# Beta in four transfers from SP and ACT, five gate copies on GpSimd, and a new order of all items

## The chip, the cores and the metric

One core of one Trainium2 chip runs the whole program. The metric is the device time of one execution in microseconds (us); the time before is the median of three runs. The core has four compute engines that are named here as the profile names them: PE (matrix products; PEld is its weight load), DVE (vector), ACT (activation functions, copies), POOL (GpSimd). SP only issues DMA transfers; ACT and POOL can issue them too. Each engine works off its own queue in the order in which the program was written, and waits there for what its next instruction needs.

## The reference

Inputs are q, k, v and g (4 batches, 8 heads, 768 steps, 48 features), beta (4, 8, 768), and two weight matrices, w_in (384 x 2048) and w_out (2048 x 384). A delta rule runs along the steps, for each of the 32 heads; its output is the input of a two-layer network with a softplus between the layers.

```
k_n = k / (norm(k, axis=-1) + 1e-06)
for t in range(S):
    y[:, :, t] = g[:, :, t] * einsum('bhd,bhde->bhe', q[:, :, t], state)
    v_old = einsum('bhde,bhd->bhe', state, k_n[:, :, t])
    state = state + beta[:, :, t] * einsum('bhd,bhe->bhde', k_n[:, :, t], v[:, :, t] - v_old)
x = y.transpose(0, 2, 1, 3).reshape(B * S, H * D)
out = softplus(x @ w_in) @ w_out
```

## The kernel before

The 768 steps are cut into 12 chunks of 64. Within a chunk the rule is solved in closed form with the inverse of a lower triangular 64x64 matrix for each head; from chunk to chunk the state is handed on. Two chunks (a pair) share one inverse: chunks 0 and 1, 2 and 3, and so on.

Every piece of work is an item of a list (`add`, line 44), with the engines that may run it, what it depends on and the buffers it uses. The table `_ORDER` at the end of the file names each item with its engine (S for SP, A, D, G for POOL, P). `emit` writes the items in just that order, so the table sets the queue of every engine, and which ring slot a buffer gets. The items that matter here, by the name they have in this text:

- load: one transfer of 192 KB, half a chunk of k, v or g (L249, 64 rows of 16 heads with 192 bytes each) or of q (L271, 128 runs of 1536 bytes). All go from SP, apart from two of k that go from ACT.
- front of a chunk (L306): casts of k and q to 16 bits (chunks 0 and 1) or k times the inverse norm (kmul, L327), transposes on PE (k at L345, q at L388), their copies out of PSUM (kev, by way of the copy helper, L218 on ACT and L220 on DVE), products of k with k and q (gram: L432, L461, L503) and copies (kkc, kdc) or masked copies (mask, L480 and L518) of those.
- norms of a pair: squares (ksq, L545, ACT), sums (red, L549, DVE), then the root: on ACT for pairs 0/1 and 2/3 (L561), as a power on POOL for the others (pow, L566); eps (L570, L572, DVE).
- inverse of a pair: beta over the squared norms (lbeta, L583 to L586, pair 0/1 only), the diagonal (diag, L621), diagonal blocks picked out (kd0, kd1 at L604) and turned around (ln, L611), two preparations (prep, L629), 15 steps (L639 and L646), all of these serial; for pair 0/1 on DVE, for the others on POOL. Then a scaling (cv, L228), transposes (tn, L667; t32, L686), and three rounds of small products: xmm (L707), tmm (L732), zmm (L770), with copies xs, tlo, thi and z between.
- chain of a chunk: ks and qs (L813), w (L847), umm (L855), u1, zu (L878), u2, smm (L898), s (the new state, L913), ymm (L928), y (times g, L943), ytr (L962), xt.
- dense layers: g1 (h, L992; for chunks 0, 1, 10 and 11 an item is 6 products 256 wide and there are 8 items a chunk), softplus (L1004, ACT), g2 (L1019, four products an item), o (copy, ACT or DVE), store (L1039, SP). There are two PSUM buffers for h and one for o.
- wload: the weights in eight quarters, w0.0 to w0.3 of w_in and w1.0 to w1.3 of w_out, issued by POOL (L297), cast to 16 bits on the way. g1 needs one quarter of w_in, g2 one of w_out.
- warm: 24 items of three idle products on the identity (L1064) that keep PE busy; they need nothing but the buffer of o.
- table: one ACT instruction (L1051) that brings the softplus table in.

Beta lies in SBUF as one row of 32 steps for each of 128 partitions and six pairs. Before, eight transfers bring it in at the start, issued by POOL (L175), 16 partitions each. They stand on POOL ahead of the mask and of the constants of xs.

The queue of POOL before, after the constants:

```
c16:0 clear:2 diag:2 tlo:0.1 tlo:0.0 w0.0 cast:q5 w0.3 w0.2 w0.1 w1.0 w1.1 w1.3 pow:4 w1.2 prep:2.0 prep:2.1 step:2.0 ...
```

A name with one number after the colon is of that chunk, or of the pair that begins with it. pow:4 belongs to chunks 4 and 5, prep:2 and step:2 to 2 and 3. eps:4 follows ln:2 on DVE.

Of the kernel before, what the change touches and what calls it, by code (L numbers as in the profile page):

```python
# [11 lines left out]
F16 = mybir.dt.float16  # L12
# [62 lines left out]
def kernel(  # L75
# [11 lines left out]
    nc = tc.nc  # L87
    B, H, S, D = q.shape
    P = 128
    C = 64  # L90
    HC = 32
    NC = S // C
# [10 lines left out]
    pool = ctx.enter_context(tc.tile_pool(name="sb", bufs=1))  # L103
# [4 lines left out]
    add = prog.add  # L108
# [59 lines left out]
    for r in range(2):  # L168
        for hf in range(2):
            l0 = 32 * (2 * r + hf)  # L170
            src = beta[2 * r : 2 * r + 2].rearrange(
                "p h (c l r) -> (p h) l c r", l=2, r=64
            )
            for cl in range(2):
                nc.gpsimd.dma_start(  # L175
                    out=beta_l[l0 + 16 * cl : l0 + 16 * cl + 16],
                    in_=src[:, cl, :, 32 * hf : 32 * hf + 32],
                )
# [59 lines left out]


# [336 lines left out]
    def inverse(cc, kk, kk_it, kkd, kd_it, nv, nv_it):  # L576
# [11 lines left out]
        if raw:  # L588
            bl_it = add("lbeta", tag, "D", lbeta, deps=[nv_it], bufs=[nv, nl, bl])
            bb = [bl]  # L590
        else:
            bl_it, bb = None, []
# [5 lines left out]
        if not raw:  # L598
# [4 lines left out]
            def kd1(en):  # L603
# [21 lines left out]
                   deps=[prev, bl_it], bufs=[tt] + bb)  # L625
# [166 lines left out]

    state = [None, []]
# [249 lines left out]
    for cc in range(NC // 2):  # L1043
        cs = [2 * cc, 2 * cc + 1]
        nv, kk = Buf(r_nv), Buf(r_kk)
        nv_it = norms(cs, nv, cc in ON_ACT)
        kkd = Buf(r_kkd)
        ka, kb = front(cs[0], kk, kkd, nv, nv_it), front(cs[1], kk, kkd, nv, nv_it)
        inverse(cc, kk, ka[0] + kb[0], kkd, ka[1] + kb[1], nv, nv_it)
    table = add("table", "", "A",  # L1050
                lambda en: nc.scalar.activation(dummy, half_c[:, :1], AF.Softplus),  # L1051
                deps=[root_last[0]])
    for c in range(NC):
        chain(c)
# [20 lines left out]
S0 D158 P1232 P1234 P1233 P1235 A1 P1236 P1238 D111 P1237 P1239 P114 A9 A104 D105 A110 P112 S8  # L1075
A106 D115 P1241 D113 P124 P121 A123 D134 P137 A138 D133 P135 P1243 D125 P147 D107 D122 A136 P144
A108 P1240 P127 P1242 A149 P1249 A148 A146 D126 P1248 D109 D156 S19 S18 A145 S2 P1250 A206 P207
S3 A116 A117 A208 P118 A120 S5 S17 A119 P150 A152 S12 A129 S33 A154 D159 S27 S26 D157 D160 D161
D162 D163 D164 D165 D166 D167 D168 D169 D170 D171 P128 S16 D172 D173 D174 P1251 D175 D176 D177
P1244 A197 S25 D198 A222 P223 A224 G179 S11 A140 D178 G238 G239 P1245 A131 P1246 P1247 S24 A199  # L1080
P181 D180 S10 A139 P184 A182 D200 S4 D588 D132 D130 G188 A185 G187 P183 A190 P193 D194 A189 A594
P595 S13 A589 S32 P590 A201 D202 D203 D219 P186 A596 A591 P597 A598 P592 P605 A593 P603 S7 S6
D606 D604 A191 P204 P609 P607 A587 S34 D192 A275 D205 P209 D608 P214 S35 S42 S43 D211 A610 D210
D216 P220 G96 A212 A217 A215 D213 P141 A221 A142 A143 D218 D276 S41 S40 A277 P600 P599 D601 D602
P195 G300 D196 P872 D278 G99 A873 P230 A231 P225 A228 P1255 A226 A233 A235 D232 D229 D227 D611
D234 P874 A875 P886 D236 P619 P612 D620 D613 P151 D155 A284 P884 G98 A887 A885 G97 S14 D237 P285
P1254 A286 P882 P301 A883 A302 P615 A616 S49 P622 A623 P876 S15 A877 P878 G100 G101 G103 P614
P617 G279 D280 P621 P624 D153 S48 A879 A625 A618 G102 D281 P282 D297 P1252 D283 P630 D631 P632
D633 P292 A293 P298 A299 P880 A881 P634 A295 G240 G241 D294 D635 G242 G243 G244 G245 G246 P1253
G247 G248 P303 A304 G249 G250 G251 G252 G253 D306 D307 S50 P308 D296 A309 A311 P904 A905 P916  # L1090
A917 D312 P287 A290 D288 A313 P914 G254 G255 G256 D305 A915 P888 P910 A911 D314 D315 P627 P626
D629 D628 A353 D257 D258 P912 A913 P908 D354 P889 G259 D260 A909 G316 G317 P906 A907 G318 G319
G320 P902 A903 P890 P891 S57 A892 S56 P261 A262 G321 A267 P264 D265 A355 P895 P896 D291 P638
P266 P263 A270 D289 P643 P636 D310 G322 P897 P898 A268 P271 D356 G357 S20 S21 D644 A269 A899
P646 A647 D637 P639 A640 P918 S51 D362 P363 D272 A364 P641 A642 P645 P648 A649 S59 S58 A378 D358
P919 P920 P921 A922 D359 P650 P651 D653 P654 D652 S22 S23 D655 P656 P273 P925 P379 D657 A380
D274 P660 P667 P658 G323 G324 G325 G326 G327 A659 P926 P669 S28 S29 D668 G375 P670 A671 S65 S64
A431 D661 P663 D664 P927 D432 P672 A673 P662 P665 A666 S31 P360 D361 P376 S30 P678 D679 A377
P680 D681 P365 A366 D367 A368 D369 P928 P682 D683 P381 D383 A384 G328 G329 G330 G331 G332 G333
P386 A389 D388 D387 P956 S72 S73 A433 D385 A957 D434 P962 P370 D371 D390 D372 A963 A373 A382  # L1100
P954 A955 P936 A937 A391 P675 S74 P674 P934 G334 A935 G335 D336 S66 D374 S67 G440 G337 D676 S894
S36 D338 D677 D392 P944 S901 A945 S923 P342 A343 D393 P339 P952 A953 S37 S44 A340 A346 P948 A949
P441 P940 A941 A345 P684 P691 D692 D685 A442 P341 P693 P344 D348 G435 D436 A347 D453 P942 A943
S75 P932 A933 P349 P687 P694 S81 S80 P686 G394 S45 D350 A509 G395 G396 G397 G456 G398 P960 G399
S924 S39 A695 A961 A929 P950 D688 P689 D690 P454 S38 A951 P946 A947 P938 S88 A939 P457 G400 A458
G401 G402 G403 G404 G405 D510 P958 A959 S89 P964 G406 G407 S893 S931 S91 P702 D703 S930 S90 P351
S54 P696 D697 D352 A511 D512 P965 P966 P967 D968 S970 G408 G409 G410 P698 A455 P459 A462 D461
D463 P699 D460 D700 P971 P972 D701 P973 P974 P464 D437 S900 P704 A975 S85 S969 P708 A465 P438
D468 A467 D466 D709 D705 P978 P715 D716 P711 A439 A712 P979 P448 D450 D452 D451 D449 P718 S47
S46 S60 G534 G411 S53 G412 A415 A719 D416 P710 P713 A714 P980 P981 P443 D445 D447 P717 P720 A982  # L1110
S52 A444 P726 D727 P985 A721 P706 A446 A469 P728 A424 D729 P722 P723 P535 A536 P730 D707 P986
P987 D731 P1000 S55 G513 A1001 P1014 A1015 D470 S83 D471 A423 P988 A989 P1008 P1010 G413 A1009
D414 P420 A1011 P417 A418 D724 D514 D725 D531 P1018 A1019 P994 A995 A421 P532 D533 D515 P998
A999 P739 P732 D733 S82 A518 P734 P419 P422 D740 G472 G473 G474 G475 D426 P1004 A1005 D425 P996
A997 P429 P427 P742 D430 A743 P735 A736 P1002 D428 A1003 P519 P741 P744 P737 G476 A745 P1020
A1021 D738 S991 S70 D520 G477 S983 P516 P1006 P750 D751 S977 A517 A1007 S69 S976 P542 D544 D545
A543 D546 P752 P992 S71 A993 D753 P1016 A1017 P521 D523 A522 D525 P746 A524 P747 S990 D748 D749
P1022 A1023 P1012 G478 G479 G480 A1013 G481 P526 D530 A527 A529 P537 A540 D539 D538 P763 D541
# [54 lines left out]
```

## Time and profile before

| | us |
|---|---|
| median of 3 runs (lowest, highest) | 256.98 (256.75, 257.29) |
| the profiled execution | 255.46 |
| its span, first to last instruction | 253.6 |

| engine | busy us | share of the span | instructions |
|---|---|---|---|
| PE | 236.9 | 93% | 5040 |
| PEld | 160.5 | 63% | 5040 |
| DVE | 153.7 | 61% | 311 |
| ACT | 153.0 | 60% | 285 |
| POOL | 127.1 | 50% | 227 |

The mean granted clock of PE was 0.966; in the slices of the span it shows as 9 (nearly full) but for the stretch from slice 5 to slice 8, where it lies between 5 and 7:

```
PEclk9999757799999999999999999999999999999999
DMA  8999999999990789083943850643024130112113
```

A slice is a fortieth of the span, 6.34 us. Where PE is busy in such slices it runs some of the time at half speed. The 16 DMA engines are nearly always busy in the first twelve slices, which is where the loads run ahead of their use. The chain that ended last is for 76% of the span work of PE, and the two dense layers alone are 25% and 23% of it.

A line of a timeline gives the start, the length, the engine, the line of the kernel, the operation, what is written and read, the shape, how many; in brackets the idle time before it and what ended it. In a table by stretch the columns are the length and then, engine by engine, the busy time and the number of instructions; the last three are the granted clock, the share of the DMA engines and GB/s.

### The profile page before, as it was taken

What the parts mean: (1) busy time and instruction counts of PE and PEld (TensorE: products, weight loads), DVE (VectorE), ACT (ScalarE), POOL (GpSimd) and SP (SyncE); (2) the same over time, 40 slices, a digit from 0 to 9 for tenths busy, and PEclk for the clock granted to TensorE, in tenths of its full rate; (3) what the DMA queues carried; (4) which work ended last, traced back from release to release, by engine and by line L of the source; (5) the groups of instructions that cost most, each with busy time, mean ns of one, the idle gap of its engine ahead of it and who ended that gap; (6) DMA issues with size and microseconds to landing.
All of it is one profiled execution on the core that took longest, in us unless ns stands there. A gap on an engine that the chain in (4) does not pass through costs nothing.

```text
span 253.6 us, 11355 instructions
## 1 busy us (share of the span) xinstructions
PE 236.9 (93%) x5040; PEld 160.5 (63%) x5040; DVE 153.7 (61%) x311; ACT 153.0 (60%) x285; POOL 127.1 (50%) x227
## 2 busy tenths in 40 slices
PE   7976588998989999999999999999999999999993
PEld 3543577676766765666766767755676565777751
DVE  7789888775893699759697588523843315313000
ACT  3557777686866579973777675456453475223530
POOL 8201653978879889988948859884000000000000
PEclk9999757799999999999999999999999999999999
DMA  8999999999990789083943850643024130112113
GB/s 111 198 181 178 178 179 180 186 195 176 176 153 6 173 180 157 4 200 83 156 98 84 170 99 22 124 83 80 3 66 93 23 80 0 34 32 48 34 47 78
DMA packets 86192, 27.56 MB, mean 109 GB/s; under 512 B 76288, under 2 KB 86144, under 8 KB 86144
## 3 DMA queue, kind: packets, MB, share of 16 engines
q1 hardware_dynamic: 80096, 23.21, 50.2%
q0 software_dynamic: 3968, 3.25, 8.2%
q10 hardware_dynamic: 2080, 0.39, 1.2%
q8 instruction: 39, 0.64, 1.2%
q14 instruction: 9, 0.07, 0.1%
HBM read 25.26 MB, written 4.72 MB: 118 GB/s over the span
## 4 chain that ended last, share of the span: by engine, by line
PE 76%; DVE 9%; DMA 4%; issue 3%; SPq 2%; ACT 2%; POOL 2%; ACTq 0%; DVEq 0%; POOLq 0%
PE h L992 25%; PE o L1019 23%; PE d L813 4%; DMA beta_l<-in_beta_dram 3%; PE d L855 3%; PE d L732 3%; PE d L770 3%; PE d L878 2%; PE d L928 2%; PE d L503 2%; PE d L707 2%; PE d L898 2%; PE d L388 2%; PE d L345 2%; POOL beta_l L175 2%
## 5 line engine op out<-in xcount | busy, mean ns | idle before, releaser
L1004 ACT ACTIVATE ga<-h 128x512 f16<-128x512 f32 x96 | 56.3, 598 | 33.4 <-PE h L992 27.6
L992 PE MATMUL h<-xt,w_in 128*128 128x512 f16 (+1 forms) x384 | 73.3, 330 | 0.1
L1019 PE MATMUL o<-w_out,ga 128*128 128x384 f16 x384 | 70.3, 326 | 1.4 <-issue 0.7
L1019 PEld LDWEIGHTS <-ga 128*128 128x128 f16 x384 | 35.7, 98 | 23.9 <-issue 1.8
L992 PEld LDWEIGHTS <-w_in 128*128 128x128 f16 x384 | 35.6, 99 | 20.7 <-issue 0.6
L639 POOL TENSOR_TENSOR tmp<-nn,tt 128x30 f32<-128x30 f32 (+7 forms) x75 | 30.1, 401 | 5.6
L646 POOL TENSOR_TENSOR tt<-tt,tmp 128x30 f32<-128x30 f32 (+7 forms) x75 | 29.4, 392 | 5.9
L566 POOL TENSOR_TENSOR nv<-nv,half_c 128x32 f32<-128x32 f32 x4 | 21.8, 5456 | 5.1 <-DVE nv L549 5.1
L218 ACT ACTIVATE kqt<-d 128x1024 f16<-128x1024 f16 (+1 forms) x21 | 18.4, 903 | 7.0 <-PE d L388 6.1
L218 ACT ACTIVATE osb<-o 128x384 f32<-128x384 f32 x18 | 8.8, 489 | 21.5 <-PE o L1019 21.4
L943 DVE TENSOR_TENSOR yg<-d,gf 128x384 f16<-128x384 f32 x24 | 12.8, 553 | 13.6 <-PE d L928 10.2
L1064 PE MATMUL o<-ident 128*128 128x512 f16 x72 | 19.3, 411 | 1.4 <-POOL ident masks.py:199 1.4
L847 DVE TENSOR_TENSOR w<-vf,d 128x384 f16<-128x384 f32 x22 | 11.3, 549 | 12.0 <-PE d L813 10.8
L218 ACT ACTIVATE u<-d 128x384 f16<-128x384 f32 x31 | 14.3, 491 | 7.1 <-PE d L878 3.3
L218 ACT ACTIVATE kk<-d 128x256 f16<-128x256 f32 (+1 forms) x34 | 12.8, 413 | 7.8 <-PE d L503 6.4
L518 DVE TENSOR_TENSOR mt<-d,mask 128x256 f16<-128x256 f32 x40 | 15.5, 418 | 3.2 <-PE d L503 1.9
L220 DVE CAST u<-d 128x384 f16<-128x384 f32 x17 | 9.1, 549 | 13.1 <-PE d L878 11.6
L813 PEld LDWEIGHTS <-kqt 48*64 48x64 f16 x704 | 13.3, 108 | 5.5 <-issue 5.3
L220 DVE COPY osb<-o 128x384 f32<-128x384 f32 x6 | 3.3, 556 | 21.6 <-PE o L1019 21.6
L813 PE MATMUL d<-s,kqt 48*64 48x48 f16 x704 | 16.4, 188 | 0.0
L545 ACT ACTIVATE ksq<-kf 128x768 f32<-128x768 f32 x12 | 10.1, 843 | 7.6 <-DMA kf<-in_k_dram 6.7
L220 POOL CAST tw<-tt 128x256 f16<-128x256 f32 x10 | 5.4, 563 | 16.1 <-DVE tt L646 16.0
(110 smaller groups left out, 380.1 us busy)
## 6 DMA issues: line engine op xcount, KB each, us to landing
qf<-in_q_dram SPq DMA_DIRECT2D x24, 192.0 KB, 5.1
vf<-in_v_dram SPq DMA_DIRECT2D x24, 192.0 KB, 5.2
gf<-in_g_dram SPq DMA_DIRECT2D x24, 192.0 KB, 4.2
out_dram<-osb SPq DMA_DIRECT2D x48, 96.0 KB, 2.4
kf<-in_k_dram SPq DMA_DIRECT2D x22, 192.0 KB, 5.1
w_in<-in_moe_w_in_dram POOLq DMA_DIRECT2D x4, 384.0 KB, 7.5
w_out<-in_moe_w_out_dram POOLq DMA_DIRECT2D x4, 384.0 KB, 12.9
kf<-in_k_dram ACTq DMA_DIRECT2D x2, 192.0 KB, 7.5
```

Of the source, the lines that this page charges most:

```text
L218: nc.scalar.activation(o, x, AF.Copy, scale=float(sign))
L220: ENG[en].tensor_copy(o, x)
L518: nc.vector.tensor_tensor(mt[c][m].ap[:, NP * p : NP * p + NP], gb[m].ap.rearrange("p (n b) -> p n b", n=NP)[:, :, C:], mask[:, None, :].b ...
L566: lambda en: nc.gpsimd.tensor_tensor(nv.ap, nv.ap, half_c, ALU.pow),
L639: eng.tensor_tensor(t, nn.ap[:, :, j + 1 :, j : j + 1].broadcast_to([P, 2, n, w]), tt.ap[:, :, j : j + 1, :w].broadcast_to([P, 2, n, w]), ...
L646: eng.tensor_tensor(rows, rows, t, ALU.add)
L813: nc.tensor.matmul(hd(o.ap)[HALF[r], NP * p + i], kq_of(c)[FEAT[m], 8 * p + 2 * i + r, off : off + C], s0[r].ap[FEAT[m], NP * p + i], **st ...
L943: lambda en, m=m: nc.vector.tensor_tensor(heads(yg.ap, m), hd(yp[m].ap), heads(gf.ap, m), ALU.mult),
L992: nc.tensor.matmul(hp.ap[:, n * b : n * b + n], w_in[:, j, f * P : (f + 1) * P], xt.ap[:, j, t0 : t0 + n], start=(j == 0), stop=(j == 2),)
L1004: lambda en, hp=hp, o=gb: nc.scalar.activation(o.ap, hp.ap, AF.Softplus),
L1019: nc.tensor.matmul(op.ap[:, :DM], b.ap[:, col + c0 : col + c0 + 128], w_out[:, f, :], start=(f == 0), stop=(f == NF - 1),)
L1064: nc.tensor.matmul(wb.ap.rearrange("p (a b) -> p a b", a=4), ident, ident[:, None, :].broadcast_to([P, 4, P]),)
```

## The change

Beta no longer comes from POOL. Four items "beta" are added, each a transfer of 32 partitions with a source pattern written by hand, and SP or ACT may issue them. The items that use beta (lbeta and diag) now depend on all four.

Five items "gate" are added on POOL. Each copies one column of a buffer (a cast k of chunk 0 and of chunk 1, the kk of chunk 0, the transposed k and q of chunks 0 and 1) into a small tile that nobody reads, and so waits until that buffer has been written.

The order table is new altogether. The items, their operations and their sizes are otherwise the same, 24 warm items among them; 92 items run on another engine than before (copies out of PSUM between ACT and DVE for the most part).

```diff
-    for r in range(2):
-        for hf in range(2):
-            l0 = 32 * (2 * r + hf)
-            src = beta[2 * r : 2 * r + 2].rearrange(
-                "p h (c l r) -> (p h) l c r", l=2, r=64
-            )
-            for cl in range(2):
-                nc.gpsimd.dma_start(
-                    out=beta_l[l0 + 16 * cl : l0 + 16 * cl + 16],
-                    in_=src[:, cl, :, 32 * hf : 32 * hf + 32],
-                )
...
+    beta_it = []
+    for r in range(2):
+        for hf in range(2):
+
+            def beta_load(en, r=r, hf=hf):
+                l0 = 32 * (2 * r + hf)
+                src = beta[2 * r, 0, 32 * hf :]
+                ENG[en].dma_start(
+                    out=beta_l[l0 : l0 + 32],
+                    in_=bass.AP(
+                        src.tensor, src.offset, [(C, 2), (S, 2 * H), (2 * C, NC // 2), (1, HC)]
+                    ),
+                )
+
+            beta_it.append(add("beta", f"{r}{hf}", "SA", beta_load))
...
-            bl_it = add("lbeta", tag, "D", lbeta, deps=[nv_it], bufs=[nv, nl, bl])
+            bl_it = add("lbeta", tag, "D", lbeta, deps=[nv_it] + beta_it, bufs=[nv, nl, bl])
...
-                   deps=[prev, bl_it], bufs=[tt] + bb)
+                   deps=[prev, bl_it] + beta_it, bufs=[tt] + bb)
...
+        if cc == 0:
+            gate_of += [(kn_it[0][-1], kn[0]), (kn_it[1][-1], kn[1]), (ka[0][-1], kk)]
+            gate_of += [(kqt_it[c][1][-1], kqt[c]) for c in cs]
...
+    gates = pool.tile([P, 8], F16, name="gates")
+    for x, (it, b) in enumerate(gate_of):
+        add("gate", f"{x}", "G",
+            lambda en, x=x, b=b: nc.gpsimd.tensor_copy(
+                gates[:, x : x + 1], b.ap.rearrange(gate_form[len(b.ap.shape)])[:, :1]
+            ),
+            deps=[it], bufs=[b])
```

What the new table makes of the queues at the start, as far as it is spoken of below (w0 to w1 are the weight quarters, warm items left out but on PE):

```
SP    k0.0 k1.0 q0.1 beta q1.0 beta beta q1.1 k2.0 q0.0 v0.0 k3.0 k2.1 ...      (before: k0.0 k1.0 q2.1 q2.0 q0.0 q0.1 v0.1 ...)
ACT   k0.1 k1.1 beta ksq:0 kev:k0.1 ksq:1 kev:k1.1 kev:k1.0 sqrt:0 six kdc, casts and kev of q0 and q1, four kkc,
      ksq:2 cast:q2 c16:0 xs xs tlo thi:0.1 ksq:3 thi:0.0 w0 sqrt:2 u1 u1 u2 u2 xt:0.1 ksq:4 kev:q2 table kev:k2 kev:q3 ...
DVE   ... cv:0 tn:0 mask mask t32:0 red:2 vs:0 w0 red:3 z:0 eps:2 cast:q3 kmul:k2 y y xt:0.0 kmul:k3 thi:1.0 red:4 kev:k3
      eight of mask and kkc (2 and 3), red:5, four more, mask:1.0 z:1 kd1:2 ln:2 s s eps:4 kmul:k5 kmul:k4 vs:1 w:1.0 kev:k5 mask:1.1 w:1.1 ...
POOL  clear:2 gate:4 w0.0 gate:1 w0.3 gate:2 tlo:0.0 w0.2 cast:q5 gate:3 w0.1 diag:2 w1.2 w1.3 w1.1 gate:0 pow:4
      prep:2.0 w1.0 prep:2.1 step:2.0 ... step:2.14 cv:2 pow:6 ...
PE    three warm, trs:k0.0 warm trs:k0.1 warm, gramd, trs:k1, gramd, gramk:0 trs:q0 trs:q1 gramq:0 warm gramk:1 five warm,
      xmm xmm trs:q2 warm tmm:0 two warm, zmm:0 umm umm zu zu ymm ymm ytr ytr trs:q3 tmm:1 trs:k2 warm trs:k3 gram:2.0 g1:0.14 ...
```

On PE the first g2 item now stands right behind zu of chunk 1 (before, behind three g1 items of chunk 1), and three g1 items of chunk 1 stand ahead of the second pair's xmm where there were eight.

## The prediction

> All times are us of the profiled execution unless said otherwise. It took 255.46 (span 253.6 and 1.9 around it); the median of the three runs shown is 256.98, so what I find is added to 256.98.
>
> **What bounds the kernel now.** First the busy time by stretch, then the slices of the granted clock.
>
> ```profile
> 24.24:51.77 27.53, 22.54 (x527) 17.96 (x525) 23.14 (x40) 20.54 (x41) 17.20 (x16) 0.69 1.13 180
> 92.88:246.00 153.12, 153.03 (x3152) 101.12 (x3152) 81.16 (x145) 89.69 (x167) 67.67 (x123) 1.00 0.39 78
> ...
> 24.59:28.00 3.41, 1.58 (x55) 1.07 (x55) 3.41 (x6) 2.13 (x5) 1.35 (x4) 1.00 0.92 139
> 28.00:31.42 3.42, 2.52 (x93) 2.35 (x87) 2.82 (x5) 2.94 (x8) 3.30 (x3) 0.50 1.14 204
> ...
> 41.66:45.07 3.41, 2.07 (x65) 1.53 (x62) 2.87 (x5) 1.88 (x4) 0.78 (x1) 1.00 1.21 191
> 45.07:48.48 3.41, 3.41 (x14) 1.93 (x15) 2.97 (x5) 2.84 (x6) 3.41 (x1) 0.50 1.26 185
> ```
>
> The columns are length, then PE, PEld, DVE, ACT, POOL busy, clock, DMA share, GB/s. From 92.88 on PE is busy for 153.03 of 153.12: nothing can be won there, since both orders hold the same 457 PE items, 24 of them idle fills. What can change lies ahead of that: the serial start, the half clock between 28.0 and 48.5, and the second inverse on POOL.
>
> ```profile
> 24.27 0.91 POOL L220 CAST tw<-tt 128x256 f16<-128x256 f32 x2 [16.03 <-DVE tt L646]
> ...
> 44.29 5.46 POOL L566 TENSOR_TENSOR nv<-nv,half_c 128x32 f32<-128x32 f32 x1 [4.02 <-DVE nv L549]
> 49.73 0.82 POOL L297 DMA_DIRECT2D w_out<-in_moe_w_out_dram  x1
> 51.86 1.20 POOL L629 TENSOR_TENSOR nn<-ln,beta_l 128x256 f32<-128x256 f16 x2 [1.32 <-DVE nv L570]
> ```
>
> POOL's own timeline: the power (L566) for pair 2 waits for DVE's reduction (L549) and takes 5.46; the inverse of chunks 2 and 3 starts at 51.86. The chain that ended last shows where it ends, and what PE loses after that:
>
> ```profile
> 5.57 7.45 DMA beta_l<-in_beta_dram
> ...
> 70.54 1.19 PE d L707 x64
> ...
> 75.28 0.75 issue
> ```
>
> The same chain begins with beta, and DVE's timeline shows its price: 0.81 of waiting at L585.
>
> ```profile
> 13.14 0.19 DVE L585 TENSOR_TENSOR bl<-beta_l,nl 128x32 f32<-128x32 f32 x1 [0.81 <-DMA beta_l<-in_beta_dram]
> ...
> 13.68 1.05 DVE L611 STREAM_TRANSPOSE ln<-kkd 128x512 f32<-128x512 f32 x1
> ```
>
> **Beta.** Eight issues leave POOL (4.53 from 1.56). POOL then idles until 24.27, so that is worth nothing. Three issues join SP, one ACT, at 0.6 to 0.8 each. ACT's comes after its two loads (end 2.55) and before the first square at 5.89: hidden there, 0.75 if not. On SP they stand ahead of q and k loads, which land 6.8 to 7.5 after issue (first four q loads): a backlog that hides 0.6 of issue. If beta comes in time, DVE reaches L585 at 12.33; then L611 waits for ACT's six kkd copies, 1.2 (four took 0.79 at 11.90) after the root, which ends at 11.5, so it starts at 12.7 to 13.0 instead of 13.68. Gain **0.7**. The bound on the other side is under the rivals.
>
> **Gates.** Five 128x1 copies; the nearest POOL rows are a 128x32 COPY at 0.24 and a 128x1 MEMSET at 0.10: 0.5 to 1.2 together, I take 1.2. POOL had 4.02 of idle time before the power, which covers them; without that cover they push it by 1.2. Their inputs (k casts, k and q evictions of chunks 0 and 1, one kk copy) are done ahead of the first L707 in the new queues, by about 25; POOL's first item there, the clear, waits for the cast and scaling of the first pair and cannot run sooner. So the gates hold little back. The first weight transfer comes at about 26 rather than 31.18, as one cast (0.91) and one scaling (1.55) leave POOL ahead of it. Behind a waiting gate stand all later transfers and the power.
>
> **Last weight quarter.** w1.0 now goes out after the first half of the pair's preparation. The transfer at 49.73 landed 9.5 later, others of w_out up to 15.8. PE needs w1.0 at the first second-layer item, about 61. With issue near 50 it is there; if it takes 15.8 it is 5 late, of which the wait named next hides 2.
>
> **Items that change engine** after 93 (output copies, evictions of the late chunks) I cost at nothing: a full PE hides them, and 0.5 each is the price where it doesn't.
>
> **Where the sum is made.** I compare both orders at one point, the products L707 of chunks 2 and 3 (70.54 before). Counted from the tables, before that point the old order has done 16 first-layer items, the new one 11 and one q transpose more; all else, and all 24 fills, are the same. An item there is 6 matmuls of h (in the chain 12 take 1.31 to 1.43, so 0.66 at least), a q transpose 0.45. So the new order stands 5 x 0.66 - 0.45 = 2.85 behind in work, and breaks even only if its L707 starts at **67.7**.
>
> Backwards from there: the old way from L629 at 51.86 to 70.54 is 18.68. The new one adds the w1.0 issue (0.82) between the two preparations and does the scaling L228 on POOL (two take 1.86 in this trace) instead of DVE (1.09): 20.27. So L629 has to start by **47.4**. It needs the power and DVE's ln (L611) of that pair.
>
> From 24.24 until that ln ended at 51.77 DVE was busy 23.14 and idle 4.39. Up to the same ln the new queue adds two casts (0.55 each) and three kk copies (0.42 each), and leaves two state copies (1.02), one v scaling (0.94) and two w (1.02) for later: 23.14 + 2.37 - 2.98 = 22.53. The first transpose L667 no longer stands behind a reduction (0.94), so the first L707 may start sooner; DVE's sum stays. It starts at 24.24 - 0.7 = 23.54. Without any idle time ln ends at 46.1, with the old idle time at 50.5. The new queues have one wait that I can name: ACT runs square (0.84), q eviction (1.02), table load (1.28 + 0.20) and k eviction (1.02) one behind the other, 4.36, before gram 2.0 can start; DVE has 3.4 of work then (copy 0.36, kmul 0.92, scale 0.47, reduction 0.94, eviction 0.69) and gram takes 0.3 to 0.5 more: 1.3 to 1.5 idle. With the old waits for z and yg (0.85 and 1.02, part of which remains) I take **3.0**: ln ends at 49.1. The power: reduction 5 stands 5.2 of DVE work before ln's end (four 256-wide ops 1.5, mask 0.66, z 0.75, kd1 1.28, ln 1.04), so 43.9, plus 5.46: 49.4. Then L707 at 49.4 + 20.3 = 69.7, **2.0 late**. PE has less in hand than it needs to cover this and stands for about 2 before it. After it I change nothing: the old order's 0.75 at 75.28 may go, and six more changes between 64-wide and full matmuls stand against it.
>
> Sum: 256.98 + 2.0 = **259.0**.
>
> **Rival 1, the clock, slower.** At 24.59:28.00 PE was busy 1.58 of 3.41 and the clock was halved for what followed; so too after 2.07 of 3.41. The new order has 9 fewer fills before the first L707 and sets three between it and the z products (after trs q2, and two behind the scaled products). At half clock a fill is 1.35, not 0.65; the scaled products 1.04, not 0.50; q2's transposes 0.85, not 0.45: 3.0 more on the path. If it bites, 262.0. For it: fewer fills; against: five of them now stand right before L707.
>
> The Trainium skill (TensorE: Matmul & The Clock Gate, section Part 1: The HAM clock gate) has the clock halved after an idle window of about 3.4 us. This trace halves it after a window that was 46% busy; by the page alone the new order would keep full clock and this rival would fall, by the trace it stays.
>
> **Rival 2, beta late, slower.** A transfer whose packets are shared by few of the 16 engines lands late and holds up what is queued behind. The page's queue counts bear on how many share one:
>
> ```profile
> q1 hardware_dynamic: 80096, 23.21, 50.2%
> q0 software_dynamic: 3968, 3.25, 8.2%
> q10 hardware_dynamic: 2080, 0.39, 1.2%
> ```
>
> q1 carried 142 transfers: 70 of k, v and g with 1024 runs each (64 rows by 16 heads), 24 of q with 128, 48 stores with 64. That is 77,824 runs; 2,272 = 142 x 16 packets are left, one closing packet for each engine: all of them were shared by 16. The new beta pattern has 2 as its outermost count. Shared by two, 96 runs of 128 bytes fall on one engine, against 64 of 192 bytes of a k load, which came about 1.1 apart: 1.1 to 1.6 a transfer, four of them. Counting on from the q loads at positions 3 to 6 of SP (landed between 9.1 and 12.0), the last beta lands near 14.4 instead of 13.02. Then the 0.7 is lost and 1.4 more: 259.0 + 2.1 = **261.1**.
>
> The Trainium skill (DMA: Bandwidth & Descriptors, section Why a DMA increments its semaphore by 16 and not by 1) says that the slowest dimension sets how many engines a transfer uses: here 2. The counts above agree for 16, and no run here yet shows a 2. By the page this rival holds; by the earliest rows beta is in time and the sum stays 259.0.
>
> **Rival 3, faster.** With full clock through 28 to 48 DVE waits less for PE. The deciding point is L629 at 47.4. With no DVE idle at all, ln ends at 46.1, the power at 46.4, L707 starts at 66.7: 1.0 gained, and 0.75 if the wait at 75.28 goes too: **255.2**. For it: the old order loses 4.39 of DVE time here and sat at half clock for 17 us. Against it: the ACT queue above, and ACT's 20.54 busy of 27.53, which leaves little to shift.
>
> **Chances.** Forecast 0.37 (own range 257.6 to 260.4); clock 0.14; beta 0.20; faster 0.29, of which 0.05 lies so near the old time that it is no change. About 0.2% (0.5) is what a measurement of this kernel can tell from none; with the low edge of the forecast that makes same 0.09, faster 0.24, slower 0.67. The range goes down to rival 3 at 255.0 and up to beta late with half the clock's price, 261.1 + 1.5, and a little: 263.0.
>
> **What would show it.** DVE's wait at L585 gone and L611 at 12.8 to 13.1 (beta right), or L585 after 14 (rival 2); SP's packets up by 3 x 208 with sixteen engines, by 3 x 194 with two. POOL's second L629 start: 49.4 forecast, 47.4 tie. Second L707 at 69.7 with about 2 of PE idle before it. Clock between 25 and 49: half or full. First weight issue near 26. The prediction is wrong if that L629 starts before 47.4, or if PE from 93 on is no longer full.

## The result, and the profile after

| | before | after |
|---|---|---|
| median us (lowest, highest) | 256.87 (255.94, 257.29), 4 runs | 267.08 (263.70, 268.38), 4 runs |
| ratio, 95% interval | | 1.0359 [1.0257, 1.0461] |
| profiled execution, its span | 255.46, 253.6 | 267.43, 265.7 |
| second L707 (after: L712) starts | 70.54 | 79.75 |
| PE busy, share of the span | 93% | 92% |

Slower by 3.6%, where 259.0 was forecast, in a range up to 263.0. The ratio leaves out runs more than 1.5% above the fastest of their kernel, so it isn't quite the ratio of the medians. The two profiled executions lie 12.0 apart, the medians 10.2; the accounts below are of the profiled ones. Most lines of the kernel after are five to seven higher (L611 is L616, L629 is L634, L707 is L712, L1019 is L1026); the copy helpers are lower (L220 is L209) and the fills (L1064) are L1081.

The loss lies ahead of 80 us. Stretches of the kernel after, with the columns of the table before (length, then PE, PEld, DVE, ACT, POOL busy, clock, DMA share, GB/s):

```profile
8.00:12.00 4.00, 4.00 (x79) 2.11 (x78) 2.31 (x6) 1.33 (x2) 0.00 (x0) 1.00 0.29 50
...
25.27:53.76 28.49, 25.29 (x535) 18.04 (x534) 21.86 (x41) 21.63 (x40) 14.52 (x17) 0.88 1.18 193
...
60.92:64.34 3.42, 0.00 (x0) 0.01 (x1) 0.48 (x2) 1.15 (x2) 2.87 (x8) 1.00 1.23 211
64.34:67.75 3.41, 2.75 (x37) 1.48 (x37) 1.42 (x4) 2.25 (x5) 2.86 (x8) 0.50 0.50 83
...
80.00:250.00 170.00, 169.78 (x3803) 114.24 (x3798) 97.68 (x178) 101.44 (x190) 81.43 (x151) 1.00 0.44 82
```

The same stretch of 8 to 12 in the kernel before:

```profile
8.00:12.00 4.00, 3.88 (x153) 2.40 (x152) 3.25 (x11) 2.20 (x6) 0.24 (x1) 1.00 1.20 210
```

From 80 on PE is full, as it was from 92.88 before. In 60.92 to 64.34 it does nothing at all, and in the 6.82 after that it runs at half clock. In 8 to 12 the core moves 50 GB/s, where it moved 210 before. The clock of 1.00 in that first line isn't a reading: the first clock record of this trace is at 26.79, and the view counts what is ahead of it as full. The lengths of PE's products show half clock there (see e4). And in the 28.49 from the last step of the first inverse to the end of the second ln DVE is busy 21.86: 6.6 idle. These are the four places to explain.

The chain that ended last, kernel after, in order of time (start, length, what):

```profile
5.48 0.67 SPq L236
6.19 3.67 SPq L236
9.91 1.22 SPq L276
...
34.85 0.51 DVE qn L209
35.38 0.56 SPq L276
...
37.30 8.90 DMA kf<-in_k_dram
46.31 0.80 ACT ksq L550
...
47.94 15.17 DMA kf<-in_k_dram
63.23 0.71 issue
63.94 1.01 ACT kqt L207
65.00 0.47 PE d L862 x8
```

It begins with beta on SP: the third beta issue alone (L236) takes 3.67, and the next load of q leaves at 9.91. It then goes by way of the cast of q chunk 3 on DVE (34.85), which frees the buffer that the load of q5 waits for, and by way of the load and the square of k chunk 5 to the last load of k chunk 6, which leaves at 47.94 and lands 15.17 later. ACT's and PE's timelines show who waits for that load:

```profile
63.19 0.84 ACT L550 ACTIVATE ksq<-kf 128x768 f32<-128x768 f32 x1 [7.49 <-DMA kf<-in_k_dram]
63.94 1.01 ACT L207 ACTIVATE kqt<-d 128x1024 f16<-128x1024 f16 x1
```

```profile
65.00 0.47 PE L862 MATMUL d<-w,te 64*64 64x48 f16 x11 [4.10 <-ACT kqt L207]
...
79.75 1.19 PE L712 MATMUL d<-tn,kk 64*64 64x32 f16 x64
```

The square of k6 stands ahead of an eviction of k4 in ACT's queue. PE needs the eviction; it doesn't need the square for a long time yet.

Three of the forecast's marks, on POOL, on DVE and in the table of queues (packets, MB, share of 16 engines):

```profile
29.24 0.99 POOL L302 DMA_DIRECT2D w_in<-in_moe_w_in_dram  x1
...
44.44 0.82 POOL L209 CAST qn<-qf 128x768 f16<-128x768 f32 x1 [10.59 <-PE d L350]
...
48.67 5.50 POOL L571 TENSOR_TENSOR nv<-nv,half_c 128x32 f32<-128x32 f32 x1
54.13 0.63 POOL L634 TENSOR_TENSOR nn<-ln,beta_l 128x256 f32<-128x256 f16 x1
```

```profile
13.60 0.21 DVE L588 STREAM_TRANSPOSE nl<-nv 128x32 f32<-128x32 f32 x1
...
14.23 0.19 DVE L590 TENSOR_TENSOR bl<-beta_l,nl 128x32 f32<-128x32 f32 x1
...
14.77 1.03 DVE L616 STREAM_TRANSPOSE ln<-kkd 128x512 f32<-128x512 f32 x1
```

```profile
q1 hardware_dynamic: 80678, 23.28, 48.8%
...
q10 hardware_dynamic: 2274, 0.42, 1.1%
```

SP's packets rose by 582 = 3 x 194 and ACT's by 194: each beta transfer is shared by two engines. Yet L590 has no wait for beta here (the root ahead of it is late). The first weight leaves at 29.24, not near 26: POOL's clear waits for the pair's cast, which in this order is ACT's, behind the late q2. The line of POOL's cast names a PE wait that had long ended; the load of q5 was issued at 35.38 and landed at 43.44.

### The profile page after: what moved, and what is told of

Its sections match the earlier page's. It is cut to its first block, busy times and chain, and to the rows that moved or that the text cites. A ratio compares the mean times of both kernels' runs of the same rounds, so it can differ in the third digit from the quotient of the medians.

```text
span 265.7 us, 11342 instructions
## 1 busy us (share of the span) xinstructions
PE 243.4 (92%) x5040; PEld 160.4 (60%) x5040; DVE 156.9 (59%) x322; ACT 151.8 (57%) x284; POOL 119.3 (45%) x214
## 4 chain that ended last, share of the span: by engine, by line
PE 65%; DMA 14%; POOL 6%; SPq 5%; ACT 3%; issue 3%; DVE 2%; DVEq 0%; ACTq 0%
PE o L1026 22%; PE h L999 19%; DMA kf<-in_k_dram 9%; DMA qf<-in_q_dram 5%; PE d L820 4%; PE d L862 2%; POOL tmp L644 2%; PE d L885 2%; POOL tt L651 2%; PE d L935 2%; SPq L276 2%; SPq L236 2%; PE d L712 2%; PE d L905 2%; PE d L775 2%
## 5 line engine op out<-in xcount | busy, mean ns | idle before, releaser
L1026 PE MATMUL o<-w_out,ga 128*128 128x384 f16 x384 | 71.0, 327 | 0.6 <-ACT osb L207 0.6
L1026 PEld LDWEIGHTS <-ga 128*128 128x128 f16 x384 | 35.3, 98 | 23.0 <-issue 0.8
L999 PEld LDWEIGHTS <-w_in 128*128 128x128 f16 x384 | 34.7, 98 | 19.2
L651 POOL TENSOR_TENSOR tt<-tt,tmp 128x30 f32<-128x30 f32 (+7 forms) x75 | 28.3, 377 | 5.9
L1081 PE MATMUL o<-ident 128*128 128x512 f16 x72 | 26.2, 509 | 1.4 <-POOL ident masks.py:199 1.4
L207 ACT ACTIVATE u<-d 128x384 f16<-128x384 f32 x34 | 16.3, 491 | 18.9 <-PE d L885 7.9
L209 DVE COPY osb<-o 128x384 f32<-128x384 f32 x12 | 6.7, 558 | 26.4 <-PE o L1026 26.4
L207 ACT ACTIVATE kqt<-d 128x1024 f16<-128x1024 f16 (+1 forms) x19 | 16.1, 866 | 5.9 <-PE d L350 4.2
L624 POOL MEMSET tt<- 128x512 f32 x4 | 2.1, 524 | 26.7 <-ACT tw L207 23.2
L207 ACT ACTIVATE kk<-d 128x256 f16<-128x256 f32 (+1 forms) x29 | 10.9, 416 | 5.6 <-DVE mt L523 2.2
L862 PE MATMUL d<-w,te 64*64 64x48 f16 x384 | 10.3, 190 | 4.1 <-ACT kqt L207 4.1
L1081 PEld LDWEIGHTS <-ident 128*128 128x128 f16 x72 | 7.7, 121 | 10.5 <-issue 6.7
## 6 DMA issues: line engine op xcount, KB each, us to landing
w_out<-in_moe_w_out_dram POOLq DMA_DIRECT2D x4, 384.0 KB, 10.2
```

Of the source, the lines that this page charges most:

```text
L207: nc.scalar.activation(o, x, AF.Copy, scale=float(sign))
L651: eng.tensor_tensor(rows, rows, t, ALU.add)
L862: nc.tensor.matmul(hd(up.ap)[HALF[r], pi], td.ap[HALF[r], 16 * cl + 2 * pi + m], w1.ap[HALF[r], pi],)
L999: nc.tensor.matmul(hp.ap[:, n * b : n * b + n], w_in[:, j, f * P : (f + 1) * P], xt.ap[:, j, t0 : t0 + n], start=(j == 0), stop=(j == 2),)
L1026: nc.tensor.matmul(op.ap[:, :DM], b.ap[:, col + c0 : col + c0 + 128], w_out[:, f, :], start=(f == 0), stop=(f == NF - 1),)
L1081: nc.tensor.matmul(wb.ap.rearrange("p (a b) -> p a b", a=4), ident, ident[:, None, :].broadcast_to([P, 4, P]),)
```

## The experiments

Three theories to begin with. **1**: beta on SP delays the loads, and they stay late. **2**: the new order does it: its queues put work that waits for a late load ahead of work that doesn't. **3**: the weight transfers, where the gates and the table now put them, slow the loads. The ratios are to runs of the kernel before on the same chip at the same time; 0.01 is 2.6 us. Orders are shown by the names in the queues.

| run | what | ratio [95%] | second L712 |
|---|---|---|---|
| after | | 1.0359 [1.0257, 1.0461] | 79.75 |
| e1 | beta on GpSimd, eight | 1.0179 [1.0107, 1.0250] | 77.08 |
| e2 | beta in 16-engine halves | 1.0339 [1.0236, 1.0442] | 80.43 |
| e3 | old order, new beta | 1.0067 [1.0027, 1.0107] | 71.01 |
| e4 | no gates | 1.0440 [1.0383, 1.0497] | 79.64 |
| e5 | k6 loads ahead of q6 | 1.0248 [1.0165, 1.0331] | 74.99 |
| e6 | square of k6 later | 1.0229 [1.0164, 1.0294] | 74.09 |
| e7 | e5 and e6 | 1.0191 [1.0103, 1.0280] | 74.30 |
| e8 | e7, beta on GpSimd, eight | 1.0133 [1.0073, 1.0193] | 73.13 |
| e9 | e8, q3 cast on ACT | 1.0115 [1.0063, 1.0167] | 73.82 |
| e10 | old order, four from GpSimd | 1.0052 [1.0019, 1.0084] | 71.03 |
| e11 | e9, fills as in the old order | 1.0113 [1.0079, 1.0146] | 72.19 |
| e12 | e11, w0.3 and w0.2 behind q5 | 1.0379 [1.0295, 1.0463] | 77.69 |
| e13 | after, w0.3 and w0.2 behind q5 | 1.0464 [1.0426, 1.0503] | 79.44 |
| e14 | e11, w0.0 behind q5 | 1.0328 [1.0269, 1.0387] | 78.09 |

### e1: beta back on GpSimd, in the new order

```diff
+    for r in range(2):            # the eight transfers of the kernel before, on nc.gpsimd
...
-                ENG[en].dma_start(out=beta_l[l0 : l0 + 32], ...)
+                pass
```

> The new order and its gates, with beta brought by the eight GpSimd transfers of the kernel before. Theory 1 (the beta transfers hold up SP: one issue took 3.67, the next load left at 9.91, and every later load is late from then on): the loads follow each other from 4 on, the first products L712 start by 27.2 instead of 28.58, the loads of k chunk 6 land before ACT needs them, and the time falls by most of what was lost, to 257 to 260. Theory 2 (the new order itself: the cast of q chunk 3 stands on DVE behind the first inverse, so the loads of q5, q6 and k6 leave late whatever beta does, and the square of chunk 6 stands ahead of a k eviction on ACT): the second of two k6 loads still lands after 60, ACT still idles over 4 there, and the time stays at 264 to 268.

262.34, which lies between the two: the four executions took 259.81, 260.61, 264.07 and 264.42. By the ratios beta's place is worth 0.018, about 4.6. In the profiled execution (264.07) ACT still waited 7.6 for k6 and PE 4.2; how much of that wait the two quicker ones have isn't shown.

### e2: sixteen engines for each beta transfer, same places

```diff
-                ENG[en].dma_start(out=beta_l[l0 : l0 + 32], in_=bass.AP(...))
+                for cl in range(2):
+                    ENG[en].dma_start(
+                        out=beta_l[l0 + 16 * cl : l0 + 16 * cl + 16],
+                        in_=src[:, cl, :, 32 * hf : 32 * hf + 32],
+                    )
```

> The new kernel with each beta transfer cut into two of 16 partitions, whose outermost count is 16, on the same queues at the same places (SP issues six, ACT two). Theory 1: what stalls SP is that two engines carry each transfer; with 16 no issue of beta is longer than about 1, SP's packets go up by 6 x 112 instead of 3 x 194, SP loses 6 x 0.6 at most instead of about 5.1, and the time is 257 to 261. Theory 2: SP may be on time, and the time stays at 264 to 268.

266.74: no better. SP's packets are 80768, 6 x 112 more than before, so all sixteen engines do share it. SP's timeline shows that it loses the time all the same:

```profile
4.55 0.58 SPq L277 DMA_DIRECT2D qf<-in_q_dram  x1
6.89 3.61 SPq L239 DMA_DIRECT2D beta_l<-in_beta_dram  x4
10.54 0.59 SPq L277 DMA_DIRECT2D qf<-in_q_dram  x1
```

No single issue is long now, but there are gaps between them, and the load of q behind beta leaves at 10.54 instead of 9.91. The core moves 43 GB/s in 8 to 12. So it isn't the two engines that make beta costly here, but that it stands on SP ahead of the loads.

Nor is it beta alone that SP holds back. In the kernel before, without beta on SP, one issue of a load took as long:

```profile
7.15 4.05 SPq L249 DMA_DIRECT2D vf<-in_v_dram  x1
```

That is SP's ninth issue, with eight loads of 192 KB sent. In the kernel after it is the seventh (6.19, 3.67), with four loads and two transfers of beta sent. In 8 to 12, while SP stands, the DMA share is 1.20 before and 0.29 after. So a reading that fits is that the engines have too few loads in hand by then; what makes SP hold an issue back isn't shown.

### e3: the old order with the new beta

```
SP before: k0.0 k1.0 q2.1 q2.0 q0.0 q0.1 v0.1 ...          ACT before: k0.1 k1.1 ksq:0 ...
SP here:   k0.0 k1.0 q2.1 beta q2.0 beta beta q0.0 q0.1 ... ACT here:   k0.1 k1.1 beta ksq:0 ...
```

> The order of the kernel before, with beta alone changed: the four transfers, one on ACT behind its two k loads, three on SP behind the first and the second of its q loads. Theory 1: SP stalls here too, the loads behind come about 4 late, and the time rises by 2 to 10, to 259 to 267. Theory 2: the old order bears it; DVE starts the first inverse a little sooner or later, and the time is within 1 of 256.9.

256.89 against 255.5: by the ratio 0.7% slower, 1.7 us, between what the two theories said. The same stall is there (the next q load leaves at 9.85, 54 GB/s in 8 to 12), and beta itself gains most of what the forecast gave it: DVE waits 0.32 for it instead of 0.81, and its ln starts at 13.13 instead of 13.68. But PE's transposes of q2 wait 4.7 for their late load and the first products start at 29.05 instead of 27.20. In the profiled execution the old order gets nearly all of it back by the second products (71.01 against 70.54).

### e4: the gates left out

```diff
-            lambda en, x=x, b=b: nc.gpsimd.tensor_copy(
-                gates[:, x : x + 1], b.ap.rearrange(gate_form[len(b.ap.shape)])[:, :1]
-            ),
+            lambda en: None,
```

> The new kernel without the five one-column copies (their output is read by nothing); all else is as it is. Theories 1 and 2: the copies took 0.2 each and the first weight transfer goes out about 0.2 earlier, three later ones about 0.2 each; the time stays at 265 to 268. Theory 3 (the gates put the weight transfers where they collide with the k6 loads): the transfers move and the time falls under 262.

267.13: nothing gained, as forecast for them. In the kernel after the five copies take 0.18 to 0.22 each. But this execution loses its time in another place. DVE's, ACT's and PE's timelines:

```profile
12.68 0.19 DVE L590 TENSOR_TENSOR bl<-beta_l,nl 128x32 f32<-128x32 f32 x1 [0.42 <-DMA beta_l<-in_beta_dram]
```

```profile
43.80 0.84 ACT L550 ACTIVATE ksq<-kf 128x768 f32<-128x768 f32 x1 [4.52 <-DMA kf<-in_k_dram]
```

```profile
48.02 0.64 PE L508 MATMUL d<-kqt 48*64 48x128 f16 x16 [4.43 <-ACT kqt L207]
```

Its start has the same order as the kernel after, but from 7.3 to 12.3 PE ran at full clock (four transposes in 0.40, in the kernel after 0.61; three fills in 0.81, there 1.49), and DVE's root came 1.95 sooner (L588 at 11.65, above at 13.60). L590 then does wait for beta, 0.42, and ln starts at 13.22. The second products come no sooner for it, at 79.64. The square of k4 now waits 4.5 for its load at the head of ACT's queue, ahead of the evictions of chunk 2 that PE waits for; DVE idles 13.2 on the way to its second ln, which ends at 59.39 instead of 53.76; and from the preparation to the second products it is 20.2, with no wait for k6. It is the same pattern, one pair of chunks earlier. So the wait for k6 isn't the only one of its kind that the new order can meet, and what the gates are worth apart from these waits isn't shown.

### e5, e6, e7: the wait for k6, from both ends

```
e5, SP:   ... g1.1 q4.0 k6.0 k6.1 q6.0 q6.1 q7.1 ...           (after: g1.1 q4.0 q6.0 q6.1 k6.0 k6.1 q7.1)
e6, ACT:  ... kev:k4 kkc:5 u1:1.1 soft kkc:5 u1:1.0 ksq:6 ...  (after: ksq:6 kev:k4 kkc:5 u1:1.1 soft kkc:5 u1:1.0)
e7:       both
```

> The new kernel with one edit: on SP the two loads of k chunk 6 stand ahead of the two of q chunk 6 instead of behind them. Theory 2a (the loads of k6 leave late because on SP they stand behind those of q6, which wait for the cast of q5 on POOL, and so fall behind three weight transfers issued within 1.6 of them): they leave by about 45 instead of 47.3 and 47.9 and land by 57 instead of 63.1; ACT's wait of 7.5 falls under 2, PE's idle 4.1 at 60 to 65 and the half clock behind it (6.8 long, so 3.4) go, and the time is 259 to 262. If the weight quarters delay them wherever they stand (theory 3), they land after 60 and the time stays at 264 to 268.

> The new kernel with one edit: on ACT the square of k chunk 6 stands five items later, behind the eviction of k chunk 4 and the two of the state that follow. Theory 2b (the late k6 hurts because the square heads ACT's queue and holds the eviction that PE waits for): k6 lands as late as before, near 63, but ACT's eviction runs near 56 instead of 63.9, PE idles under 1.5 in 60 to 65 and keeps its clock; the time is 258 to 262. If other work waits for k6 just as long (DVE's sum of it, POOL's power behind it), the wait moves there and the time stays over 264.

> Both edits together on the new kernel: k6 loads ahead of q6 loads on SP, the square of k6 five items later on ACT. Theory 2: they heal the same wait, so together no more than the better one alone, 257 to 261. Theory 1 (the late start of all loads is what costs): no edit at 45 to 60 heals it, and the time stays over 263.

262.93, 262.82 and 262.37: 0.8 to 1.4 above what theory 2 said, and below what theory 1 said for e7. (The square passes six items of ACT's queue, as the list shows.) PE's timeline of e6, where the 4.1 and the half clock had been:

```profile
59.68 0.42 PE L508 MATMUL d<-kqt 48*64 48x128 f16 x16 [1.06 <-DVE kqt L209]
60.03 0.82 PE L1081 MATMUL o<-ident 128*128 128x512 f16 x3
60.78 0.37 PE L862 MATMUL d<-w,te 64*64 64x48 f16 x12
```

L862 starts at 60.78 instead of 65.00 and the clock stays full. In e5 ACT's wait for k6 is 0.73:

```profile
56.72 0.84 ACT L550 ACTIVATE ksq<-kf 128x768 f32<-128x768 f32 x1 [0.73 <-DMA kf<-in_k_dram]
```

Either edit takes 4.8 to 5.7 off the second products, and the two together no more than one: it is one wait, that needs both the late load and the order on ACT. (e5's profiled execution lost 3.4 later by a stretch of half clock, 77.0 to 83.8.)

### e8: both edits, and beta on GpSimd

> Both edits and beta brought by the eight GpSimd transfers of the kernel before. Beta on POOL took 4 to 5 off the new kernel by itself and the wait for k6 was still there (ACT 7.6, PE 4.2). If the two costs add, the time is 262.3 less 6 to 8: 254 to 257, level with or below the kernel before. If the same time was counted twice, it stays at 258 to 262.

260.71, so "the same time counted twice": with the wait healed, beta's place is worth 0.006 (1.0191 to 1.0133, about 1.5), as in the old order (1.7), and not the 4.6 of e1. The two costs hang together: a late load stream is dear where a queue waits for it. Every execution of e8 was quicker than every one of e7, though the intervals overlap. Two stretches of e8, and its marks on POOL and PE:

```profile
9.75:13.17 3.42, 2.51 (x170) 1.78 (x168) 2.14 (x8) 2.69 (x10) 0.00 (x0) 1.00 1.29 177
13.17:16.58 3.41, 1.03 (x8) 0.77 (x8) 3.14 (x11) 2.28 (x7) 0.00 (x0) 0.50 1.50 155
...
24.21:52.76 28.55, 25.29 (x523) 18.38 (x524) 21.80 (x41) 21.20 (x39) 14.96 (x17) 0.76 1.15 194
```

```profile
53.11 0.61 POOL L638 TENSOR_TENSOR nn<-ln,beta_l 128x256 f32<-128x256 f16 x1
```

```profile
73.13 1.19 PE L716 MATMUL d<-tn,kk 64*64 64x32 f16 x64 [1.23 <-DVE tn L676]
```

From the preparation to the products it is 20.0 here (20.3 was forecast). But the preparation still starts 3.7 later than the forecast 49.4: DVE idles 6.75 on the way to its second ln where 3.0 was forecast, and the first inverse ends 0.7 later than forecast.

### e9: the cast of q3 off DVE

```
ACT: ... xs xs tlo cast:q3 thi ...   DVE: ... z:0 eps:2 kmul:k2 ...   (after: DVE ... z:0 eps:2 cast:q3 kmul:k2 ...)
```

> The kernel with both edits and beta on GpSimd (260.7), with the cast of q chunk 3 moved from DVE (35.2, behind z and the normalisation) to ACT behind the second scaling of the first pair (ACT idled 1.7 there, from 28.9). Theory 2: that cast holds the q ring, so the loads of q5 leave near 30 instead of 35.7, POOL casts q5 near 36 instead of 41.5, and DVE has 0.5 less to do before its second ln; the second L716 comes 0.5 to 1.5 sooner than 73.1 and the time is 259 to 260.5. Theory 3: the weight transfers behind that cast then leave near 37 and meet the loads of k5; the power starts no sooner and the time stays at 260 to 262.

260.25, which fits both, but the second products come at 73.82, later than in e8 and not sooner as theory 2 said. The loads of q5 leave at 29.96 and 33.89 as theory 2 said, but take 11.4 and 8.3 and land at 41.3 and 42.2, no sooner than in e8. Three weight quarters, issued at 27.1, 28.0 and 30.9, travel beside them. So theory 3 has a part.

### e10: the old order, four transfers from GpSimd

```diff
-            for cl in range(2):
-                nc.gpsimd.dma_start(out=beta_l[l0 + 16 * cl : l0 + 16 * cl + 16], ...)
+            nc.gpsimd.dma_start(out=beta_l[l0 : l0 + 32], in_=bass.AP(...))    # the new pattern
```

> The kernel before with beta in the four new transfers of 32 partitions, but issued by GpSimd, where eight stood. If two engines for one transfer are what makes beta slow (rival 2 as predicted), the last lands after 13 and DVE's wait of 0.8 for beta stays or grows: 256.5 to 258.5. If SP's queue is what made it costly, the last is issued 2 sooner (3.6 instead of 5.6), lands by 12, DVE's wait goes, the first ln starts at 12.7 to 13.1 instead of 13.7, and the time is 255.5 to 257.

257.73 against 256.56, 0.5% slower. POOL's and DVE's timelines:

```profile
1.67 5.01 POOL L172 DMA_DIRECT2D beta_l<-in_beta_dram  x4 [0.30 <-issue]
```

```profile
14.93 0.19 DVE L593 TENSOR_TENSOR bl<-beta_l,nl 128x32 f32<-128x32 f32 x1 [1.50 <-DMA beta_l<-in_beta_dram]
```

Four issues take 5.01 where eight took 4.53, the last transfer lands at 14.81 instead of 13.02, and DVE waits 1.50 instead of 0.81. With SP out of it, this is what rival 2 forecast: the new pattern, and beta late. That few engines carry it here too isn't shown by the packets: GpSimd's queue has 3968 in both kernels.

### e11: the fills where the old order has them

```
PE: ... five warm, warm warm warm xmm xmm trs:q2 tmm:0 zmm:0 ...   (after: five warm, xmm xmm trs:q2 warm tmm:0 warm warm zmm:0)
```

> The kernel of e9 with three groups of idle fills that the new order put between the first products and z (one behind q2's transposes, two, 2.74 long at half clock, ahead of the z products) moved ahead of the first products, where the old order has them. Rival 1 (the clock): with more fills there PE is busy before the products and keeps its clock from 26 on, z comes about 2 sooner, and with it DVE, the power and the second L716 by 1 to 2: 258 to 259.5. If what binds there is the power's input (the square of chunk 5, whose k load leaves at 37) and not z, the second L716 stays within 0.7 of e9's and the time too.

259.47. In the profiled executions the second products come 1.6 sooner than in e9 (72.19 against 73.82), as rival 1 said; the ratios (1.0113, 1.0115) don't tell the two apart.

### e12, e13, e14: the weights later

```
e12, e13, POOL: clear gate:4 w0.0 gate:1 gate:2 tlo cast:q5 w0.3 w0.2 gate:3 w0.1 ...
e14, POOL:      clear gate:4 gate:1 w0.3 gate:2 tlo w0.2 cast:q5 w0.0 gate:3 w0.1 ...   (after: w0.0, w0.3, w0.2 ahead of cast:q5)
```

> The kernel of e11 with two of the three early weight transfers (issued at 28.3 and 31.2 there) behind the cast of q5 on POOL, where the old order has them. In e9 the loads of k4, v2 and q5, issued at 27 to 34, took 8 to 12 each beside those transfers; loads of the old order issued at 27 to 30 took 5 to 6. Theory 3: without the weights there k4 lands by 34 and q5 by 37, POOL casts q5 by 38, the second L716 comes 1 to 2 sooner than 72.2, and the time is 257 to 258.5. If the transfers then meet the loads of k5 (issued near 36) instead, the square of k5 and the power come no sooner and the time stays at 259 to 260.

> The new kernel with that one edit: the transfers w0.3 and w0.2 behind the cast of q5 on POOL; beta, the q3 cast, the k6 loads and the square of k6 as in the new kernel. Theory 3 (the early weights are the root of the late k6): q5 lands by 40 instead of 43.4, the loads of q6 and k6 leave 3 sooner, k6 lands by 58 and the time is 258 to 263. Theory 2 (the queues' order): the weights merely move against k6, which still lands after 61, and the time stays at 264 to 268.

> The kernel of e11 with only the transfer w0.0 behind the cast of q5 on POOL; w0.3 and w0.2, which the first two first-layer items read, stay early (moving them made PE wait 4.3 for w_in). If early weights against the loads of k4 and q5 are what is left of the loss (theory 3), k4 lands by 36 and q5 by 40, w0.0 is there when the third first-layer item reads it, the second L716 comes about 1 sooner than 72.2 and the time is 258 to 259. If the products have to wait for w0.0 instead (over 1 at w_in), the new order has no place for its weights that hurts neither: 259.5 to 263.

265.92, 267.45 and 264.44: worse than without the edit, or the same. e12 and e14 lie above everything that was expected of them. e13 lies where theory 2 put it, but not for its reason. The loads did come sooner (in e12 q5 landed at 38.0 instead of 42.4), and in e13 ACT's wait for k6 was gone. But PE's timeline of e13 shows a new wait of the same size (4.34 in e12, 4.48 in e14):

```profile
48.45 1.46 PE L999 MATMUL h<-xt,w_in 128*128 128x256 f16 x6 [5.33 <-DMA w_in<-in_moe_w_in_dram]
```

The new order's first first-layer items read w0.3, w0.2 and w0.0 one after the other. Transfers issued behind q5's cast land 6 to 9 later, too late for them. Early, they slow the loads that POOL, ACT and DVE wait for. No run found a place that hurts neither, and none of the runs beats the kernel before.

## Why the prediction was wrong

**The way of counting held.** The forecast compared both orders at the second products and said that the new one breaks even at 67.7, since it has 2.85 less work of PE done there. Span less the start of those products is 183.1 before and in e3 (184.7 in e10). In the new order it is 186.0 in the kernel after and 185.7 to 186.3 in e4, e6 to e9 and e11 to e14: 2.6 to 3.2 more. (It is 185.3 in e1, 185.6 in e2 and 188.9 in e5, which has half clock behind them.) So 79.75 - 67.7 = 12.05 late, and the span grew by 12.1.

**The steps that failed** are those that put the products at 69.7. They came 10.05 later in the profiled execution, in three parts that add up:

| step | forecast | measured | us |
|---|---|---|---|
| last step of the first inverse ends | 23.54 | 25.27 | 1.7 |
| from there to the end of ln:2: busy 22.53 + idle 3.0 | 25.5 | 28.49 | 3.0 |
| from L634 to the second L712 | 20.3 | 25.6 | 5.3 |

The parts tell where this execution lost its time; they aren't prices that could each be had back. In e4 the first inverse ends 1.6 sooner (23.71) and the wait for k6 is gone, and the second products come at 79.64 all the same. By the ratios, the two edits of e7 are worth 0.017, beta's place behind them 0.006, and about 0.011 is left in e11.

**The missing term, 5.3.** The sum followed one chain backwards from the products (preparation, power, DVE) and looked at SP's queue at its head alone. It said of PE that it "has less in hand than it needs", put about 2 of standing ahead of the products, and named no wait for a load of k between 47 and 70. The load of k6, issued behind q6's, behind q5's cast, behind q3's cast, was in no term, nor was the square that waits for it on ACT. In e6 to e8, where the wait is healed, that stretch measures 20.0 to 20.3, so the rest of this step was right.

**The idle time of DVE, 3.0 forecast.** It was 6.6 in the kernel after and 6.75 in e8, which has beta on GpSimd: more than the old order's 4.39. Busy time was 0.7 under the forecast. The waits are those that were named (kqt 1.4, yg 1.6) and those that weren't (the sum for chunk 3 behind ACT's square 1.1, xt 1.0), part of them behind PE work at half clock. This was a term with the right cause and half its size.

**The start, forecast as 0.7 gained.** ln starts at 14.77, 1.1 later than before. DVE doesn't wait for beta here, as the term asked, but that is luck: the root is late. With the root at its old time DVE waits 0.3 (e3) and 0.4 (e4), and ln starts 0.5 sooner than before, not 0.7. SP's "backlog that hides 0.6 of issue" hides nothing: SP loses from 6.19 to 9.86. What made ln late in this execution is PE at half clock at the start: with the same order at full clock (e4) it starts at 13.22.

**Rival 1, the clock**, was right in kind and wrong in place. It priced 25 to 28. In all thirteen of its profiled executions the new order has half clock somewhere between 8 and 27 (e8 above from 13.17); the old order, once at full clock, keeps it until 28.0 before, 24.8 in e3 and 20.1 in e10. The Trainium skill (TensorE: Matmul & The Clock Gate, section Part 1: The HAM clock gate) says that the window is free-running and doesn't begin with the kernel; e4 and the kernel after, whose work on PE is the same up to 7.3 and whose clock is not from there on, agree.

**Rival 2, beta late**: the two engines are shown by the packets, as the Trainium skill (DMA: Bandwidth & Descriptors, section Why a DMA increments its semaphore by 16 and not by 1) has it. But its price, beta later than before, isn't what happened on SP and ACT: the last beta packet there started at 12.14, and DVE's waits of 0.3 and 0.4 (e3, e4) are shorter than the 0.81 before. It is what happened on GpSimd (e10). On SP the price is the loads behind, 1.5 to 1.7 where nothing waits for them (e3; e7 against e8) and up to 4.6 where something does (e1).

**Rival 3, faster**: its condition came in good part. Between 28.0 and 48.5 the kernel after has 6.8 of half clock (37.0 to 43.9) where the kernel before has 17.1. Yet DVE idled more on the way to its second ln, 6.6 against 4.39. More clock by itself didn't take those waits away.

**Right**: the size of the gates (0.99 together, forecast 0.5 to 1.2), PE full afterwards, the sign. **Right by luck**: w1.0 in time. It left at 54.70 and landed at 64.98, well after the 61 that the forecast named, and met no wait because the first second-layer item was late too (71.70). In e11, with less time lost, PE waits 0.7 for it.

**Open**: why SP holds issues back, with beta on it or without, and how much of the last 1.1% is the weights against the loads. e12 to e14 moved that wait without removing it.

## What to carry to other kernels

Break-even counted in work at one point of the schedule is worth its trouble: it gave the span of eleven of the thirteen profiled executions of the new order to within 0.4 (e1: 0.7 off, e5: 3.0). Then walk every queue from its head to that point, not only the chain that ends there, and ask at each instruction that waits for a transfer what stands behind it. In a start where loads bind, small transfers that stand ahead of them on the same issuing queue cost loads, even if they themselves arrive nearly in time.

## What the runs showed of the hardware

- Transfers of beta in 128-byte runs, 24 KB each, ahead of 192 KB loads on SP: 50 GB/s in 8 to 12 with two engines for each transfer, 43 with sixteen, 54 in the old order, 210 and 190 with beta issued by GpSimd (before, e8). One issue took 3.67; the kernel before, with loads alone on SP, has one of 4.05.
- From GpSimd, a transfer of the new pattern (32 partitions, e10) takes 1.2 to 1.4 an issue and lands 8.2 to 9.4 after it; one of the old pattern (16 partitions, before) 0.5 to 0.8 and 4.6 to 7.5.
- A load of 192 KB issued between 13 and 25.5 took 4.3 to 6.2 in the kernel before, with no weights beside it. Beside the first weight quarters, loads issued between 27 and 34 took 7 to 12 in e8 and e9, and one took 15.2 in the kernel after with four quarters under way. The kernel before has such loads too: 15.4 and 19.5, issued at 37.1 and 38.2 behind weights.
- The clock was halved after windows of 3.4 us in which PE was busy 0.00 (60.92 to 64.34 of the kernel after), 1.34 (33.62 to 37.03 of the kernel after) and 2.51 (9.75 to 13.17 of e8, shown above).
